# Clustered attention and two MLPs on one core: which engine copies which transposes, and when ScalarE converts weights

## The chip, the core and the metric

The kernel runs on one core of one Trainium2 chip. A core has TensorE (PE in the profile, its weight loads PEld), VectorE (DVE), ScalarE (ACT), GpSimd (POOL) and SyncE (SP), each with a queue of its own that runs in order, and 16 DMA engines. The metric is the device time of one execution in microseconds.

## The reference, cut to what matters

```
q, k, v: (2, 8, 768, 64);  centroids: (8, 16, 64)
q_assign, k_assign = argmax of normalized q, k times normalized centroids
scores = q k^T / 8, and -1e9 where the two assignments differ
attn   = softmax(scores);  x = attn v, reshaped to (1536, 512)
h = x @ w_in (512 x 2048);   x = (h * sigmoid(h)) @ w_out
gate = sigmoid(x @ w_gate (512 x 1536));  val = x @ w_val
out = (gate * val) @ w_out2 (1536 x 512)
```

The weights come as 64-bit floats and are turned into 32-bit floats on the chip. All results are fp32.

## The kernel before

**Attention.** The 16 heads are handled in eight pairs p of two heads j, and the 768 queries of a head in six tiles i of 128; one pair is thus twelve tiles, called 0 to 11 below. `one_tile` runs two tiles ahead with `scores`: four matmuls into one of two PSUM buffers `s`, VectorE's maximum over the row (L462), and ScalarE's exponential into `e` (L467), which also sums. `transposes` (L481 and L492) then turns the 128 x 768 block of `e` by six TensorE transposes: two go into a tile `u` that two query tiles share, four into a tile `t`. Both kinds of tile come from one PSUM pool of three buffers. A copy moves them to the SBUF tile `ph`; it is written in the helper `cast`, so its line is L64 on ScalarE and L67 on VectorE. VectorE copies each shared `u`. After every third tile `values` (L500) multiplies by v for the three tiles before; ScalarE copies one half of the result (`other`, L509) and VectorE adds the other (L512). `finish_last` scales the last pair's result into `acc`.

**Weights.** A job makes the operands of one weight block. `converted` loads 64-bit words (L687), and turns them into floats by ScalarE (L692), GpSimd (L693) and three steps of bits on VectorE (L698, L700, L702). `two` splits a float into a high part, cast by ScalarE (again L64), and the rest, subtracted by GpSimd (L710). `seven` makes the seven operands of a Strassen scheme: GpSimd forms the sums `si` and `two` splits them, for the first block into `wi0a`, `wi0b`, `wi0s`, `wi0t`. `plain` makes a block of the output weights (`wo`). The jobs stand in one list: first hidden block, its two output blocks, second hidden block, and so on. `weights(key)` traces a job and the two behind it.

**MLPs.** `hidden` runs a hidden block of the first MLP by Strassen's scheme in steps x, w, X, y, z, v, W; the first block runs it for one half of the tokens and `hidden_directly` for the other. `mixed` multiplies by the output weights; in its first pass ScalarE copies the product to `acc` (L901), and in later ones VectorE adds (L903). The second MLP follows in the same manner.

**What sets the order.** In the long loops TensorE's instructions keep the order of the code (`manual_schedule`). For the other engines a planner decides from simulated times and the order of the code which ready instruction comes next, and so it does for the PSUM buffer that a tile gets; the chip then runs each queue in that order. `tc.issue_after(ins)` keeps the instructions of a block behind `ins`, if they are on the engine of `ins`. `begin` holds the exponential of the last pair's first tile; `ends` the last value copy L509 (and a matmul). `behind` does this for VectorE's bit steps of the first four conversions.

The code that the diff touches:

Of the kernel before, what the change touches and what calls it, by code (L numbers as in the profile page):

```python
# [14 lines left out]
AF = mybir.ActivationFunctionType  # L15
# [16 lines left out]
def clustered_attention_then_two_mlps(ctx, tc, qT, kT, v, cen, cenT, w1i, w1o, w2g, w2v, w2o, out):  # L32
    nc = tc.nc
    B, HP, _, S = qT.shape
# [10 lines left out]
    NPAIR = B * HP  # L45
# [3 lines left out]
    GT = G // P  # L49
# [6 lines left out]
    ends = []  # L56
    begin = []
    maxima = []
    copied = []
    home = {0: xp}  # L60

    def cast(eng, o, i):
        if eng is nc.scalar:
            return nc.scalar.activation(o, i, AF.Copy)  # L64
        if eng is nc.gpsimd:
            return nc.gpsimd.tensor_scalar(o, i, 1.0, 1.0, op0=ALU.mult, op1=ALU.mult)
        return nc.vector.tensor_copy(o, i)  # L67
# [41 lines left out]
    with ExitStack() as att:  # L109
# [339 lines left out]
        def scores(p, j, i):  # L449
            qa, qm, ka, km, _ = heads[p]  # L450
            s = ps_s.tile([P, 2, 512], F32, tag="s", name=f"s{p}_{j}_{i}")
            for n, (a, c) in enumerate(((qa, ka), (qm, km))):
                for g in range(2):
                    nc.tensor.matmul(  # L454
                        s[:, g, 0:HS],
                        lhsT=a[:, j, i * P : (i + 1) * P],
                        rhs=c[:, j, g * HS : (g + 1) * HS],
                        start=n == 0,
                        stop=n == 1,
                    )  # L460
            nm = sm.tile([P, 1], F32, tag="nm", name=f"nm{p}_{j}_{i}")
            maxima.append(nc.vector.tensor_reduce(nm, s[:, :, 0:HS], axis=AX.XY, op=ALU.max, negate=True))  # L462
            e = wk.tile([P, 2, HS], F32, tag="e", name=f"e{p}_{j}_{i}", bufs=4)
            if p not in tots:
                tots[p] = fin.tile([P, 2 * NT], F32, tag="tot", name=f"tot{p}")
            n = j * NT + i
            x = nc.scalar.activation(e, s[:, :, 0:HS], AF.Exp, bias=nm, scale=1.0, accum_out=tots[p][:, n : n + 1])  # L467
            if (p, j, i) == (NPAIR - 1, 0, 0):
                begin.append(x)
            prob[p, j, i] = e  # L470

        ring = wk.tile([P, NT, S], F32, tag="ph", name="ph", bufs=1)
# [2 lines left out]
        def transposes(p, j, i):  # L475
            e = prob.pop((p, j, i)).rearrange("p a b -> p (a b)")
            if i % 2 == 0:
                shared[0] = ps_t.tile([P, 2, 2, P], F32, tag="t", name=f"u{p}_{j}_{i}")
            both = shared[0]
            for kt in (4, 5):  # L480
                nc.tensor.transpose(both[:, kt - 4, i % 2, :], e[:, kt * P : (kt + 1) * P], ident)  # L481
            if i % 2:
                copied[:] = [
                    cast(
                        nc.vector,
                        ring[:, 4:6, (i - 1) * P : (i + 1) * P],
                        both.rearrange("p k i q -> p k (i q)"),
                    )
                ]
            t = ps_t.tile([P, 4, P], F32, tag="t", name=f"t{p}_{j}_{i}")  # L490
            for kt in range(4):
                nc.tensor.transpose(t[:, kt, :], e[:, kt * P : (kt + 1) * P], ident)  # L492
            eng = nc.vector if i % GT == 1 and p < NPAIR - 1 else nc.scalar
            cast(eng, ring[:, 0:4, i * P : (i + 1) * P], t)

        def values(p, j, g):
# [102 lines left out]
        for t in tiles[:2]:  # L599
            scores(*t)  # L600
# [57 lines left out]
        for i in (NT - 2, NT - 1):  # L658
            transposes(p, 1, i)
# [23 lines left out]
    def converted(src, name):  # L683

        r = rp.tile([P, KD * P], mybir.dt.int64, tag="r", name=f"r{name}")
        with tc.issue_after(loaded[0].ins):
            nc.sync.dma_start(r, src)  # L687
        words = r.bitcast(I32).rearrange("p (n w) -> p n w", w=2)
        low, up_ = words[:, :, 0], words[:, :, 1]
        t = wp.tile([P, KD * P], F32, tag="c", name=f"c{name}")  # L690
        ti = t.bitcast(I32)
        nc.scalar.activation(t, up_.bitcast(F32), AF.Copy, scale=2.0**-112)  # L692
        nc.gpsimd.tensor_scalar(t, t, LARGEST, -LARGEST, op0=ALU.min, op1=ALU.max)  # L693
        def one():
            return tc.issue_after(behind.pop(0).ins) if behind else nullcontext()

        with one():
            nc.vector.tensor_scalar(ti, ti, 3, None, op0=ALU.logical_shift_left)  # L698
        with one():
            nc.vector.scalar_tensor_tensor(ti, low, 29, ti, op0=ALU.logical_shift_right, op1=ALU.bitwise_or)  # L700
        with one():
            nc.vector.scalar_tensor_tensor(ti, up_, SIGN, ti, op0=ALU.bitwise_and, op1=ALU.bitwise_or)  # L702
        return t

    def two(src, name, pool=None):

        w = (pool or sp[next(taken) % NSP]).tile([P, 2, src.shape[1]], R32, tag="w", name=f"w{name}")
        hi, lo = w[:, 0], w[:, 1]
        cast(nc.scalar, hi, src)
        nc.gpsimd.tensor_tensor(lo, src, hi, op=ALU.subtract)  # L710
        return hi, lo

    def plain(src, name):
        return two(converted(src, name), name)

    def four(srcs, name):

# [9 lines left out]
    def part(pair, n):  # L727
        return [h[:, n * Q : (n + 1) * Q].rearrange("p (k c) -> p k c", k=KQ) for h in pair]

    def seven(srcs, name, all_four=False):  # L730

        a, b = (converted(src, f"{name}_{n}") for n, src in enumerate(srcs))
        a11, a12, a21, a22 = a[:, 0:Q], a[:, Q:], b[:, 0:Q], b[:, Q:]
        first = two(a, f"{name}a")
        t = wp.tile([P, 4, Q], F32, tag="s", name=f"s{name}", bufs=1)
        sub = nc.gpsimd.tensor_tensor
        sub(t[:, 0], a21, a22, op=ALU.add)
        sub(t[:, 1], t[:, 0], a11, op=ALU.subtract)
        sub(t[:, 2], a11, a21, op=ALU.subtract)
        sub(t[:, 3], a12, t[:, 1], op=ALU.subtract)  # L740
        s12 = two(t[:, 0:2].rearrange("p a b -> p (a b)"), f"{name}s")
        s34 = two(t[:, 2:4].rearrange("p a b -> p (a b)"), f"{name}t")
        last = two(b, f"{name}b") if all_four else two(a22, f"{name}d", dp)
        made = dict(
            a11=part(first, 0),
            a12=part(first, 1),
            s1=part(s12, 0),
            s2=part(s12, 1),
            s3=part(s34, 0),
            s4=part(s34, 1),  # L750
            a22=part(last, 1 if all_four else 0),
        )
        if all_four:
            made["a21"] = part(last, 0)
        return made

    jobs, place = [], {}

    def job(key, make, *args):
        place[key] = len(jobs)  # L760
        jobs.append(partial(make, *args))

    def flat(w):
        return w.rearrange("p k c -> p (k c)")

    for i in range(N1):
        job(("1i", i), seven, [flat(w1i[2 * i + n]) for n in range(2)], f"i{i}", i == 0)
        for e in range(2):
            job(("1o", i, e), plain, w1o[i, e], f"o{i}_{e}")
    for i in range(N2):  # L770
        job(("2g", i), seven if i else four, [flat(w2g[2 * i + n]) for n in range(2)], f"g{i}")
        job(("2v", i), seven if i else four, [flat(w2v[2 * i + n]) for n in range(2)], f"v{i}")
# [1 line left out]
            job(("2o", i, k), plain, flat(w2o[2 * i + k]), f"u{i}_{k}")  # L774

    AHEAD = 2
    made = {}

    def weights(*key):

        n = place[key]
        for c in range(n, min(n + AHEAD + 1, len(jobs))):
            if c not in made:
                with tc.issue_after((ends if c > AHEAD else begin)[0].ins):
                    made[c] = jobs[c]()
        return made[n]

# [95 lines left out]
    def hidden(i, bs, order="xyzwXvW"):  # L883
        def take(c, m, h, bs, inside):
            g = c if inside else temporary(f"g{i}_{m}{h}{bs.start}")[:, bs]
            nc.scalar.activation(g, c, AF.Silu)
            split(g, m, (h, bs), f"a{i}", nc.gpsimd if m and h else nc.vector)

        yield from strassen(weights("1i", i), f"h{i}", take, bs, order)
# [8 lines left out]

    def accumulate(z, o, first):
        if first:  # L900
            nc.scalar.activation(z, o, AF.Copy)  # L901
        else:
            nc.vector.tensor_tensor(z, o, z, op=ALU.add)  # L903

# [125 lines left out]
    def steps(main, beside=iter(()), n=None):  # L1030

        for _ in main:
            next(beside, None)
            if n is not None:
                n -= 1
                if n == 0:
                    return
# [26 lines left out]
    for q in ("21", "22"):  # L1064
        right_quarter("x", 1, q, ACT, DVE)
    front = hidden(0, ONE[0], "xwXyzvW")
    steps(front, n=6)
    following = hidden_directly(0, 1)
    next(following)
    run(front)  # L1070
# [90 lines left out]
```

## Time and profile before

| | |
|---|---|
| median of three runs | 783.1 us (782.8 to 783.15) |
| profiled execution | 783.0 us, span 781.1 us |
| TensorE busy | 765.1 us, 98% (weight loads 83%) |
| VectorE, ScalarE, GpSimd busy | 80%, 52%, 51% |
| TensorE's clock granted | full, in all 40 slices |
| TensorE's longest waits in total | 4.2 us for the exponential (18 times), 1.4 for ScalarE's copies to acc |

A row of the timeline has the start from the beginning of the span, the length, the engine, the line, the operation with output and inputs, the shape and how many were merged. In brackets stand the idle time of the engine ahead of it and what ended it. Buffer numbers are left out of names: `s`, `t`, `u`, `v` are PSUM tiles of attention, `e` the exponentials, `ph` the transposed ones, `ci` and `co` the floats of hidden and output weights, `ri` and `ro` their loaded words. A row of the busy table has a stretch, its length, and the busy time and number of instructions of each engine.

### The profile page before, as it was taken

The page shows a single profiled execution, that of the slowest core. Times are in us where ns is not written, and L with a number is a line of the kernel's source. Part 1 is how long each engine was busy: PE and PEld are TensorE (multiplying, and loading weights), DVE is VectorE, ACT ScalarE, POOL GpSimd, SP SyncE. Part 2 cuts the span into 40 slices and gives each one's busy share as a digit, 9 for nine tenths or more (in the row PEclk, how much of TensorE's full clock was granted, in tenths as well). Part 3 has the DMA queues.
Part 4 walks back from the last instruction along what each step waited for, and adds up shares of the span by engine and source line. Part 5 has one row for each costly group of instructions (what it writes and reads, how often), then busy time and mean ns, then how long its engine had stood idle before and what let it go on. Part 6 is the DMA issues. An engine that isn't in the chain of part 4 may idle for free.

```text
span 781.1 us, 11455 instructions
## 1 busy us (share of the span) xinstructions
PE 765.1 (98%) x4314; PEld 651.9 (83%) x4314; DVE 626.9 (80%) x787; ACT 403.1 (52%) x690; POOL 396.2 (51%) x345
## 2 busy tenths in 40 slices
PE   8999999999998999999999999999999999999998
PEld 4666776666766988989989989998998989899896
DVE  6887887787777989979678678998497896979746
ACT  6767777777785754615525326546532425333120
POOL 5234223556654776646546326445663847748220
PEclk9999999999999999999999999999999999999999
DMA  7675466367221132222121211221021221112004
GB/s 215 154 184 146 120 164 167 111 150 196 81 75 55 54 134 83 81 81 81 55 81 55 81 55 55 81 76 58 31 81 55 81 82 54 55 68 68 1 0 162
DMA packets 25487, 71.60 MB, mean 92 GB/s; under 512 B 4484, under 2 KB 4952, under 8 KB 25432
## 3 DMA queue, kind: packets, MB, share of 16 engines
q1 hardware_dynamic: 24888, 70.84, 30.7%
q8 instruction: 34, 0.56, 0.3%
q14 instruction: 21, 0.17, 0.1%
q10 hardware_dynamic: 544, 0.03, 0.0%
HBM read 48.01 MB, written 3.19 MB: 66 GB/s over the span
## 4 chain that ended last, share of the span: by engine, by line
PE 79%; DVE 9%; ACT 6%; issue 2%; DMA 2%; POOL 1%; SPq 0%; ACTq 0%; POOLq 0%; DVEq 0%
PE z L982 12%; PE v L500 7%; PE s L454 7%; PE t L492 4%; PE h_0w L807 3%; PE h_0x L807 3%; ACT e L467 3%; PE g_0w L807 2%; PE g_0x L807 2%; PE u L481 2%; PE y_00None L923 2%; PE v_0w L807 2%; PE v_0x L807 2%; PE r L873 2%; PE q L873 2%
## 5 line engine op out<-in xcount | busy, mean ns | idle before, releaser
L462 DVE TENSOR_REDUCE nm<-s 128x1 f32<-128x768 f32 x96 | 91.5, 954 | 18.6 <-PE s L454 18.0
L467 ACT ACTIVATE e<-s,nm 128x768 f32<-128x768 f32 x96 | 86.5, 901 | 28.2 <-DVE nm L462 27.4
L982 PE MATMUL z<-wu,ghb 128*128 128x512 f32 (+1 forms) x292 | 89.7, 389 | 0.5 <-DVE acc L903 0.5
L500 PE MATMUL v<-ph,vv 128*64 128x384 f32 x384 | 69.2, 494 | 0.3 <-DVE ph L67 0.3
L982 PEld LDWEIGHTS z<-wu,ghb 128*128 128x128 f32 x292 | 54.0, 188 | 12.5 <-issue 1.3
L454 PE MATMUL s<-ka,qa 128*128 128x384 f32 x192 | 57.6, 380 | 4.3 <-ACT e L467 4.2
L492 PE MATMUL t<-ident,e 128*128 128x128 f32 x384 | 58.1, 274 | 0.3
L982 PE MATMUL z<-wu,glb 128*128 128x512 f32 (+1 forms) x146 | 57.0, 391 | 0.0
L531 POOL TENSOR_TENSOR acc<-xf,rb 128x768 f32<-128x768 f32 x7 | 12.8, 1835 | 82.6 <-DMA rb<-d_rb 82.6
L64 ACT ACTIVATE ph<-t 128x512 f32<-128x512 f32 x68 | 40.6, 599 | 21.7 <-PE t L492 20.9
L500 PEld LDWEIGHTS v<-ph,vv 128*64 128x64 f32 x384 | 25.2, 136 | 30.6 <-issue 22.9
L454 PE MATMUL s<-k,q 128*128 128x384 f32 x192 | 49.8, 339 | 0.1
L903 DVE TENSOR_TENSOR acc<-z,acc 128x1024 f32<-128x1024 f32 (+2 forms) x32 | 36.6, 1154 | 13.6 <-PE z L982 12.9
L492 PEld LDWEIGHTS t<-ident,e 128*128 128x128 f32 x384 | 43.9, 140 | 2.4 <-ACT ph L64 2.2
L481 PEld LDWEIGHTS u<-ident,e 128*128 128x128 f32 x192 | 22.8, 140 | 26.2 <-issue 19.2
L67 DVE COPY ph<-u 128x512 f32<-128x512 f32 x48 | 32.8, 684 | 12.7 <-PE u L481 12.7
L481 PE MATMUL u<-ident,e 128*128 128x128 f32 x192 | 38.8, 283 | 1.1 <-ACT ph L64 1.1
L454 PEld LDWEIGHTS s<-ka,qa 128*128 128x128 f32 x192 | 28.9, 190 | 9.8 <-ACT e L467 9.0
L710 POOL TENSOR_TENSOR wo<-co,wo 128x512 fp32r<-128x512 f32 x16 | 23.2, 1452 | 23.8 <-ACT wo L64 23.7
L454 PEld LDWEIGHTS s<-k,q 128*128 128x128 f32 x192 | 34.5, 188 | 0.8 <-ACT k L333 0.3
L982 PEld LDWEIGHTS z<-wu,glb 128*128 128x128 f32 x146 | 27.4, 188 | 7.3 <-DVE glb L863 1.8
L923 PE MATMUL y<-gha,wo 128*128 128x384 f32 x128 | 32.8, 334 | 0.0
(626 smaller groups left out, 2133.0 us busy)
## 6 DMA issues: line engine op xcount, KB each, us to landing
ri<-in_w1i SPq DMA_DIRECT2D x16, 512.0 KB, 3.2
ro<-in_w1o SPq DMA_DIRECT2D x16, 512.0 KB, 3.3
ka<-kh SPq DMA_DIRECT2D x32, 192.0 KB, 3.9
rg<-in_w2g SPq DMA_DIRECT2D x12, 512.0 KB, 3.2
rv<-in_w2v SPq DMA_DIRECT2D x12, 512.0 KB, 3.1
ru<-in_w2o SPq DMA_DIRECT2D x12, 512.0 KB, 3.3
qq<-in_qT SPq DMA_DIRECT2D x8, 384.0 KB, 3.3
kk<-in_kT SPq DMA_DIRECT2D x8, 384.0 KB, 4.8
```

What stands on the lines that cost most here:

```text
L64: return nc.scalar.activation(o, i, AF.Copy)
L67: return nc.vector.tensor_copy(o, i)
L454: nc.tensor.matmul(s[:, g, 0:HS], lhsT=a[:, j, i * P : (i + 1) * P], rhs=c[:, j, g * HS : (g + 1) * HS], start=n == 0, stop=n == 1,)
L462: maxima.append(nc.vector.tensor_reduce(nm, s[:, :, 0:HS], axis=AX.XY, op=ALU.max, negate=True))
L467: x = nc.scalar.activation(e, s[:, :, 0:HS], AF.Exp, bias=nm, scale=1.0, accum_out=tots[p][:, n : n + 1])
L481: nc.tensor.transpose(both[:, kt - 4, i % 2, :], e[:, kt * P : (kt + 1) * P], ident)
L492: nc.tensor.transpose(t[:, kt, :], e[:, kt * P : (kt + 1) * P], ident)
L500: m = nc.tensor.matmul(o[(L, U)[kt % 2]], lhsT=vv[:, j, kt, :], rhs=ring[:, kt, g * G : (g + 1) * G], start=n < 2, stop=n >= NT - 2,)
L807: nc.tensor.matmul(o[:, b, 0:HS], lhsT=w[a][s][:, k, :], rhs=right[b, q][t][:, k, :], start=start and k == 0 and n == 0, stop=k == KQ - 1 ...
L903: nc.vector.tensor_tensor(z, o, z, op=ALU.add)
L923: nc.tensor.matmul(o[:, d, 0:width], lhsT=s[:, d, k, :], rhs=t[:, c], start=k == 0 and m == 0, stop=k == 1 and m == 2,)
L982: nc.tensor.matmul(o[:, a, c], lhsT=s[:, q * P : (q + 1) * P], rhs=r[:, c], start=k == 0 and m == 0, stop=k == 1 and m == 2, skip_group_ch ...
```

## The change

VectorE copies the `t` tile of query tiles 1 and 3 of each half pair instead of 1 and 4; the others stay with ScalarE, and in the last pair all do. For the first hidden block the casts of the two operands of sums are put behind the latest exponential, which is the last one when they are traced. For the first block's output weights the high casts are put behind the last value copy, and their two jobs are traced after the first step of the first hidden block instead of ahead of all of them. All ScalarE instructions of the third hidden block's job are put behind the latest copy L901 traced by then, the last of the first output pass; before, they stood behind the value copy.

```diff
-    copied = []
+    copied, latest, firsts = [], [], []
...
             x = nc.scalar.activation(e, s[:, :, 0:HS], AF.Exp, bias=nm, scale=1.0, accum_out=tots[p][:, n : n + 1])
...
+            latest[:] = [x]
...
-            eng = nc.vector if i % GT == 1 and p < NPAIR - 1 else nc.scalar
+            eng = nc.vector if i in (1, GT) and p < NPAIR - 1 else nc.scalar
             cast(eng, ring[:, 0:4, i * P : (i + 1) * P], t)
...
-    def two(src, name, pool=None):
+    def two(src, name, pool=None, after=()):
...
-        cast(nc.scalar, hi, src)
+        with tc.issue_after(after[0].ins) if after else nullcontext():
+            cast(nc.scalar, hi, src)
         nc.gpsimd.tensor_tensor(lo, src, hi, op=ALU.subtract)
...
-    def plain(src, name):
-        return two(converted(src, name), name)
+    def plain(src, name, after=()):
+        return two(converted(src, name), name, after=after)
...
-        s12 = two(t[:, 0:2].rearrange("p a b -> p (a b)"), f"{name}s")
-        s34 = two(t[:, 2:4].rearrange("p a b -> p (a b)"), f"{name}t")
+        after = latest if all_four else ()
+        s12 = two(t[:, 0:2].rearrange("p a b -> p (a b)"), f"{name}s", after=after)
+        s34 = two(t[:, 2:4].rearrange("p a b -> p (a b)"), f"{name}t", after=after)
...
-            job(("1o", i, e), plain, w1o[i, e], f"o{i}_{e}")
+            job(("1o", i, e), plain, w1o[i, e], f"o{i}_{e}", () if i else ends)
...
     AHEAD = 2
+    look = [0]
...
-        for c in range(n, min(n + AHEAD + 1, len(jobs))):
+        for c in range(n, min(n + look[0] + 1, len(jobs))):
             if c not in made:
-                with tc.issue_after((ends if c > AHEAD else begin)[0].ins):
+                behind_it = firsts if c == place["1i", 2] else ends if c > AHEAD else begin
+                with tc.issue_after(behind_it[0].ins):
                     made[c] = jobs[c]()
...
         if first:
-            nc.scalar.activation(z, o, AF.Copy)
+            firsts[:] = [nc.scalar.activation(z, o, AF.Copy)]
...
-    steps(front, n=6)
+    steps(front, n=1)
+    look[0] = AHEAD
+    weights("1i", 0)
+    steps(front, n=5)
```

## Rows read from the trace of the kernel before

**Rows 1.** Timeline, 79.4 to 82.2 us, a first half pair.
```profile
79.52 0.96 DVE L462 TENSOR_REDUCE nm<-s 128x1 f32<-128x768 f32 x1 [0.15 <-PE s L454]
...
80.28 0.60 ACT L64 ACTIVATE ph<-t 128x512 f32<-128x512 f32 x1 [0.39 <-PE t L492]
80.39 0.68 DVE L67 COPY ph<-u 128x512 f32<-128x512 f32 x1
...
80.78 0.90 ACT L467 ACTIVATE e<-s,nm 128x768 f32<-128x768 f32 x1
...
80.94 0.43 PEld L492 LDWEIGHTS t<-ident,e 128*128 128x128 f32 x4
80.99 0.96 DVE L462 TENSOR_REDUCE nm<-s 128x1 f32<-128x768 f32 x1
...
81.82 0.30 PEld L454 LDWEIGHTS s<-ka,qa 128*128 128x128 f32 x2 [0.45 <-ACT e L467]
...
82.05 0.90 ACT L467 ACTIVATE e<-s,nm 128x768 f32<-128x768 f32 x1 [0.28 <-DVE nm L462]
```

**Rows 2.** Timeline, 92 to 96 us, a second half pair.
```profile
93.20 0.96 DVE L462 TENSOR_REDUCE nm<-s 128x1 f32<-128x768 f32 x1 [0.23 <-PE s L454]
...
94.08 0.68 DVE L67 COPY ph<-u 128x512 f32<-128x512 f32 x1
...
94.35 0.90 ACT L467 ACTIVATE e<-s,nm 128x768 f32<-128x768 f32 x1
...
95.39 0.30 PEld L454 LDWEIGHTS s<-ka,qa 128*128 128x128 f32 x2 [0.45 <-ACT e L467]
```

**Rows 3.** Timeline, 231 to 237 us, the end of attention.
```profile
231.46 0.68 ACT L692 ACTIVATE co<-ro 128x512 f32<-128x512 f32 x1 [1.06 <-POOL wi0b L710]
...
232.15 0.63 ACT L64 ACTIVATE wi0s<-si 128x512 fp32r<-128x512 f32 x1
...
232.69 0.89 ACT L467 ACTIVATE e<-s,nm 128x768 f32<-128x768 f32 x1
...
233.57 0.62 ACT L64 ACTIVATE wi0t<-si 128x512 fp32r<-128x512 f32 x1
...
234.21 0.49 ACT L509 ACTIVATE other<-v 64x384 f32<-64x384 f32 x1
...
236.80 2.16 PE L500 MATMUL v<-ph,vv 128*64 128x384 f32 x12 [0.28 <-DVE ph L67]
```

**Rows 4.** Timeline, 243 to 251 us, the first hidden block.
```profile
243.88 1.25 ACT L64 ACTIVATE wo<-co 128x512 fp32r<-128x512 f32 x2 [3.44 <-DVE co L702]
243.92 0.94 SPq L687 DMA_DIRECT2D ri<-in_w1i  x2
...
246.21 1.00 PEld L807 LDWEIGHTS h_0x<-x,wi0a 128*128 128x128 f32 x6 [0.80 <-ACT h_0u L828]
...
247.19 0.66 ACT L692 ACTIVATE ci<-ri 128x512 f32<-128x512 f32 x1 [1.04 <-DMA ri<-in_w1i]
...
250.10 1.01 PEld L807 LDWEIGHTS h_0v<-xt,wi0b 128*128 128x128 f32 x6 [0.82 <-DVE h_0u L830]
```

**Rows 5.** Busy time by stretches, the one from 246 to 299 us.
```profile
246.00:299.00 53.00, 50.24 (x283) 48.92 (x284) 48.49 (x53) 36.26 (x57) 36.48 (x31) 1.00 0.26 92
```

**Rows 6.** Timeline, 277 to 299 us, the second hidden block.
```profile
277.41 0.67 ACT L692 ACTIVATE ci<-ri 128x512 f32<-128x512 f32 x1 [1.94 <-DMA ri<-in_w1i]
...
278.82 0.43 DVE L698 TENSOR_SCALAR ci<-ci 128x512 int32<-128x512 int32 x1 [0.67 <-POOL ci L693]
...
282.73 1.28 POOL L710 TENSOR_TENSOR wi2a<-ci,wi2a 128x512 fp32r<-128x512 f32 x1
282.80 1.50 DVE L698 TENSOR_SCALAR ci<-ci 128x512 int32<-128x512 int32 x1 [1.14 <-POOL ci L693]
283.34 2.04 PEld L807 LDWEIGHTS h_0z<-xt,wi1t 128*128 128x128 f32 x12 [1.74 <-ACT acc L901]
...
298.82 0.47 PE L923 MATMUL y_00None<-gha,wo 128*128 128x512 f32 x1 [0.64 <-DVE h_0u L846]
```

## The prediction

> **What bounds the kernel now.** The page's first part comes first: TensorE is busy for nearly the whole span, VectorE for four fifths, ScalarE for half. So little can be won, and only in the idle time of TensorE. The second part shows it at full clock in every slice, so the clock is no term here. The view of waits for TensorE is second: its idle time is one wait repeated in the attention stage, the score matmuls waiting for an exponential, and single waits around the first hidden block. The timeline of all engines at these places is third, and the busy table by stretches last.
>
> The repeated wait has a chain that can be read off one place. Scores go into two PSUM buffers, so the scores of tile 7 of a pair of heads (twelve tiles, 0 to 11) need the exponential of tile 5. The maximum of tile 5 runs on VectorE from 79.52 to 80.48, ScalarE copies the fourth tile's transposes from 80.28 to 80.88, the exponential starts only at 80.78 and runs 0.90, and the weight load of the scores follows at 81.82 after 0.45 of idling [rows 1]. An exponential whose ScalarE is free starts 0.10 behind its maximum (81.95 to 82.05); this one starts 0.30 behind it [rows 1]. The second half of each pair repeats it for tile 11: maximum done at 94.16, exponential at 94.35, so 0.19 behind [rows 2]. These two places come back at the same offsets in every pair from the second to the seventh; in the first pair only the second place waits, and in the eighth all these copies stay on ScalarE.
>
> At the end of attention the exponential of tile 10 of the last pair starts at 232.69, behind two weight conversions on ScalarE (231.46, 0.68 and 232.15, 0.63); a third (233.57, 0.62) stands between it and the value copy at 234.21, and the value product that waits on this chain starts at 236.80 [rows 3]. Next ScalarE holds two output-weight casts that wait 3.44 for VectorE, from 243.88 to 245.13; the value copy and the first hidden block's copy queue behind them, and TensorE idles 0.80 at 246.21. Then ScalarE waits 1.04 for a weight load that was issued at 243.92, and VectorE's sum comes late: 0.82 at 250.10 [rows 4]. (These are the weight-load rows; the matmul rows give somewhat less, since their ends are modelled.)
>
> From 246 to 299 VectorE is busy 48.49 of 53.00 us [rows 5]. TensorE's waits there are mostly VectorE's backlog seen from the other side. The largest, 1.74 at 283.34, is a PSUM bank that ScalarE releases late, since its queue stood 1.94 at a weight conversion waiting for its load (277.41). The next, 0.64 at 298.82, is VectorE's queue itself [rows 6].
>
> **The change, part by part.** The sum is made against the profiled execution, 783.0 us (span 781.1 and 1.9 around it); the median of the runs is 783.1.
>
> *The transposes' copies.* In each half pair VectorE copied tiles 1 and 4 of six; now it copies 1 and 3, and ScalarE takes 4. The counts stay, so no engine gets more work; what moves is place. ScalarE is free when tile 5's maximum ends, and the exponential starts 0.10 behind it: 0.30 - 0.10 = 0.20 in six pairs, and 0.19 - 0.10 = 0.09 in seven second halves. 6 x 0.20 + 7 x 0.09 = 1.8 us, on the path, since the scores follow that exponential 0.14 later both times [rows 1, 2]. The cover has to be checked on VectorE: after the maximum it copies the pair of shared transposes (80.39 to 81.07) and now tile 3's behind it, to 81.75 with the same 0.68. That pushes the next maximum (80.99) by 0.7 at most; its exponential is needed only behind the value product that comes next. But the transposes of the next tile need one of three PSUM buffers. Now they start at 80.94, 0.06 behind ScalarE's copy. With that copy gone the first buffer free is the shared one, 81.07 + 0.06 = 81.13, and with 0.43 for the four loads the scores could start at 81.56, where the new exponential allows 81.62. In the second half it is 94.76 + 0.06 + 0.43 = 95.25 against 95.30. So the saving just fits. The best case is no more: maximum and exponential in sequence set it. The other end is a rival.
>
> *Two casts behind the last exponential.* Without the cast at 232.15 the exponential starts 0.64 earlier (0.09 before the end of the conversion ahead of it, as it does now), and without the one at 233.57 the value copy gains another 0.64. Sum 1.28. The value product at 236.80 hangs on this chain through VectorE's queue [rows 3]. The casts go behind tile 11's exponential, where ScalarE and GpSimd have gaps; their first user is the block ahead of 246.21, over five us later. Taken: 1.3. If the conversion at 231.46 also leaves (its job is now traced later), another 0.7 goes; if the planner puts other conversions in the gap, 0.
>
> *Output-weight casts behind the last value copy.* This frees the copy of the first hidden block, so the 0.80 at 246.21 can go, and the 0.82 at 250.10 with it if the split of the attention result starts earlier. I price this at nothing beyond the shift of 1.3, because that split (ScalarE, behind 247.19) waits for a load issued when VectorE finishes the output weights' bit operations [rows 4], and these are shifted by 1.3, not removed. Upper end 0.80 + 0.82 = 1.6; below nothing by the collision weighed next.
>
> A gap that the casts leave may be filled by their GpSimd halves. The same VectorE shift of 128x512 words took 0.43 at 278.82 and 1.50 at 282.80, where it began 0.07 behind a GpSimd subtraction of 1.28 and ended 0.3 behind it [rows 6]. So one GpSimd subtraction can cost VectorE 1.07, and the two that move may land on the bit operations ahead of 243.92: up to 2.1. The Trainium skill (SBUF — State Buffer, Who interferes with whom) says that the port pair the two share is locked for a whole instruction by whichever starts first; this row agrees, and by that rule the edit puts work on VectorE's own path. The front's lower end is 1.3 - 2.1 = -0.8.
>
> *Third job's conversions behind the second layer's copies.* ScalarE then releases the bank as soon as its product is done, and the 1.74 at 283.34 goes. But the next stop is the wait at 298.82, which VectorE sets [rows 6]. VectorE's own idle time between is 0.67 and 1.14, both ahead of conversion steps that need loads; the conversion at 277.41 itself moves back about 0.9. One sum (about 0.9) can now slip into the 1.14, less about 0.5 for the later conversion: 0.4 taken. Ends: 1.74 + 0.64 = 2.4 if VectorE's backlog dissolves, 0 if nothing slips in. So the 1.74 mostly turns into a longer wait at 298.82.
>
> Sum: 1.8 + 1.3 + 0.4 = 3.5; 783.0 - 3.5 = 779.5. Nothing behind 299 has a reason to change: there the same jobs run in the same order, and what is gained is carried along.
>
> **The rivals.**
> *Everything pays.* VectorE's backlog between 246 and 299 shrinks with the earlier start: 1.8 + 1.3 + 1.6 + 2.4 = 7.1, so 775.9. For it: 4.5 us of idle VectorE in that stretch [rows 5]. Against: its idle is ahead of loads, not of TensorE.
> *The front is swallowed.* The collision above, or conversions planned into the gap, take the 1.3: 783.0 - 1.8 - 0.4 = 780.8, and 781.6 with the whole 2.1.
> *The edit does not reach the exponential.* The planner may set another ScalarE instruction in the freed slot, or VectorE's maximum may come later: the 1.8 stays away, and with the front swallowed too only 0.4 is left, 782.6. Against: the slot holds nothing else now.
> *Slower: the transposes wait for VectorE's second copy.* If the fifth tile's transposes get the buffer of the fourth tile, they wait for 81.75 + 0.06, scores at 82.24 instead of 81.82, +0.42; in the second half 94.76 + 0.68 + 0.06 + 0.43 = 95.93 instead of 95.39, +0.54. 6 x 0.42 + 7 x 0.54 = 6.3 lost in place of 1.8 won: 783.0 + 6.3 - 1.7 = 787.6. It decides from a copy that ends later than about 81.33. For it: the saving has only some 0.05 us of room. Against: buffers are now taken in the order in which they come free, not in fixed rotation (at 80.94 one freed at 80.88, with the shared one still in use until 81.07) [rows 1].
>
> **How the numbers follow.** Forecast 779.5: 0.50, own range 778.3 to 780.6. Everything pays: 0.13. Front swallowed: 0.18. No reach: 0.11. Slower: 0.08. A measurement of this kernel tells about 0.2% from no change, 1.6 us, so faster means under 781.4 or so: 0.50 + 0.13 + 0.13 of the swallowed case = 0.76. Within: the rest of that case and most of no reach, 0.15. Slower 0.09. The range 776.2 to 782.8 leaves out the slower rival and the far half of the best one.
>
> **What would show it.** Right: the score waits of six first halves shrink from 0.45 to about 0.25 and a pair takes 0.3 less; the value product stands 1.3 earlier against the scores of tile 11; the wait at the bank of 283.34 is gone and the one before the second layer's second pass has grown. Wrong: transposes of the fifth tile start over 0.4 behind the shared copy; a VectorE row of the output weights' bit operations over 1.4 long; the time from the last exponential to the second layer's second pass as long as now, or over 4 us shorter.

## The result, and the profile after

The changed kernel is slower: median 788.17 us (786.99 to 788.51, four runs) against 783.12 (782.8 to 783.16) before, ratio 1.0063 [1.0045, 1.008]. The profiled execution took 788.4, span 786.6. The forecast was 779.5. The first 295 us went better than forecast; then one stop of TensorE and what followed it gave back twice what had been won. In the names below `p` is the product of the half of the tokens that the first block multiplies directly, `gha` and `gla` are the high and the low part of a Silu's result, and `y_00` is the first product of the second layer's second pass. A negative shift is earlier.

```
start of the same work on TensorE   before   after    shift
transposes, end of attention        235.37   231.38   -3.99
first hidden block, h_0v            250.10   244.81   -5.29
direct products p                   251.28   247.39   -3.89
second hidden block, h_0z           283.34   278.45   -4.89
third hidden block, h_0x            293.86   288.85   -5.01
third hidden block, h_0y            295.94   295.90   -0.04
second layer, y_00                  298.82   300.86   +2.04
y_00, seven products on             300.62   303.69   +3.07
third hidden block, h_0z            315.36   319.93   +4.57
```

The first edit did what it should. The timeline of the changed kernel at the place of [rows 1], and two rows at that of [rows 2]:

```profile
78.53 0.96 DVE L462 TENSOR_REDUCE nm<-s 128x1 f32<-128x768 f32 x1 [0.16 <-PE s L454]
...
79.41 0.68 DVE L67 COPY ph<-u 128x512 f32<-128x512 f32 x1
...
79.52 0.90 ACT L467 ACTIVATE e<-s,nm 128x768 f32<-128x768 f32 x1 [0.62 <-DVE nm L462]
...
80.14 0.42 PEld L493 LDWEIGHTS t<-ident,e 128*128 128x128 f32 x4 [0.19 <-DVE ph L67]
...
80.57 0.30 PEld L454 LDWEIGHTS s<-ka,qa 128*128 128x128 f32 x2
...
93.55 0.42 PEld L493 LDWEIGHTS t<-ident,e 128*128 128x128 f32 x4 [0.31 <-DVE ph L67]
...
93.98 0.30 PEld L454 LDWEIGHTS s<-ka,qa 128*128 128x128 f32 x2
```

The exponential starts 0.03 behind its maximum (79.49 to 79.52). The scores at 80.57 wait for nothing now; the transposes ahead of them wait for the shared copy, 0.05 behind its end (80.09), as reckoned. From one tile's scores to the next it was 1.81 and is 1.56 in first halves and 1.66 in second halves, so a pair takes 0.4 less. Behind the last of these places, at 209 us, the scores stand 2.85 earlier (208.51 before, 205.66 now). Of that 0.25 was there at the scores of 14.96 us already (14.71 now), ahead of the first copy that moved, so the edit gave 2.6.

The front, at the place of [rows 3, 4]:

```profile
230.22 0.49 ACT L510 ACTIVATE other<-v 64x384 f32<-64x384 f32 x1
...
232.80 0.20 PEld L501 LDWEIGHTS v<-ph,vv 128*64 128x64 f32 x4 [0.27 <-DVE ph L67]
...
241.58 0.99 PEld L812 LDWEIGHTS h_0x<-x,wi0a 128*128 128x128 f32 x6
...
243.40 0.66 ACT L693 ACTIVATE ci<-ri 128x512 f32<-128x512 f32 x1 [0.83 <-DMA ri<-in_w1i]
...
245.56 1.28 ACT L891 ACT_TABLE_LOAD   x1
...
246.85 0.49 ACT L891 ACTIVATE g<-h_0x 128x384 f32<-128x384 f32 x1
...
247.39 4.44 PE L878 MATMUL p<-x,wi0a 128*128 128x384 f32 x24 [1.38 <-ACT g L891]
```

Value copy and value product stand 3.99 and 4.00 earlier. The last scores of attention stood 2.88 earlier (232.70 before, 229.82 now), so the front brought 1.1 up to there, a little less than the 1.28 of the forecast. The stalls of 0.80 and 0.82 went as well, and at h_0v the front has 2.4. But p now waits 1.38 for the first Silu, and 1.0 is left. That Silu stands on ScalarE behind the conversion that waits for its load; directly ahead of it stands a table load of ScalarE of 1.28, which the kernel before has at the same place and which no run here moved.

The place that decides, ScalarE, VectorE, GpSimd and TensorE around [rows 6]:

```profile
274.88 0.63 ACT L64 ACTIVATE wo<-co 128x512 fp32r<-128x512 f32 x1 [2.84 <-DVE co L703]
275.41 2.20 ACT L906 ACTIVATE acc<-y 128x768 f32<-128x768 f32 x3
277.49 1.41 ACT L693 ACTIVATE ci<-ri 128x512 f32<-128x512 f32 x2
...
278.45 2.24 PE L812 MATMUL h_0z<-xt,wi1t 128*128 128x384 f32 x12
...
278.90 0.43 DVE L699 TENSOR_SCALAR ci<-ci 128x512 int32<-128x512 int32 x1 [4.05 <-POOL ci L694]
...
288.99 2.31 POOL L868 TENSOR_TENSOR gla<-h_0d,gha 128x768 fp32r<-128x768 f32 x1
...
291.25 1.44 POOL L740 TENSOR_TENSOR si<-si,ci 128x256 f32<-128x256 f32 x1
...
293.27 0.63 ACT L64 ACTIVATE wo<-co 128x512 fp32r<-128x512 f32 x1 [2.01 <-DVE co L703]
...
295.23 0.62 ACT L64 ACTIVATE wi2s<-si 128x512 fp32r<-128x512 f32 x1
...
295.90 1.65 PE L812 MATMUL h_0y<-xt,wi2s 128*128 128x384 f32 x4 [4.81 <-ACT wi2s L64]
...
296.61 1.46 POOL L712 TENSOR_TENSOR wi2s<-si,wi2s 128x512 fp32r<-128x512 f32 x1
...
298.13 2.93 PE L812 MATMUL h_0y<-xt,wi2s 128*128 128x384 f32 x8 [0.58 <-POOL wi2s L712]
...
300.86 0.63 PE L928 MATMUL y_00None<-gha,wo 128*128 128x512 f32 x1
```

The bank wait of 1.74 at h_0z is gone, as meant. Both conversions now stand behind the eighth copy; VectorE, whose bit steps follow them, idles 4.05. What stands last in this chain is the operand wi2s: GpSimd forms its sum (L740) behind the 2.31 of another block's subtraction. The sum is done at 292.69, but the cast comes only at 295.23, since ScalarE stands 2.01 at a cast wo that waits for VectorE, and then runs two more instructions first. The low part ends at 298.07, and TensorE waits 4.81 and 0.58. The busy table of the changed kernel (stretch, length, busy time and instructions of PE, PEld, DVE, ACT, POOL; then the granted clock, DMA share, GB/s):

```profile
246.00:299.00 53.00, 45.73 (x254) 44.57 (x254) 46.67 (x50) 34.52 (x54) 33.08 (x28) 0.95 0.21 70
...
273.00:286.00 13.00, 12.50 (x72) 12.18 (x72) 8.74 (x12) 5.95 (x10) 4.00 (x4) 1.00 0.28 92
286.00:299.00 13.00, 7.61 (x37) 6.79 (x36) 12.20 (x10) 9.78 (x16) 12.61 (x11) 0.78 0.24 82
...
296.00:303.00 7.00, 6.42 (x18) 5.43 (x19) 6.93 (x8) 2.42 (x4) 5.71 (x5) 0.50 0.08 14
```

Against [rows 5] TensorE and GpSimd did less in the 53 us. GpSimd's share is the telling one: 4.00 of 13 us to 286, then 12.61 of 13. And the clock, full throughout before, is at 0.50 from 296 to 303, so at 1.2 in place of 2.4 GHz, right behind TensorE's long idle stretch. From h_0x to h_0z TensorE loses 9.6 us against the kernel before: 4.97 at the wait for the cast, 2.08 to the start of y_00 (0.58 of waiting and slow products, less the 0.64 that was waited there before), 1.03 in y_00, 1.50 at h_0z, which now waits 1.34 for VectorE's sum. Over the whole span the loss is 5.5 (781.1 to 786.6).

### The profile page after: what moved, and what is told of

It is laid out like the page before. It is cut to its first block, busy times and chain, and to the rows that moved or that the text cites. A ratio compares the mean times of both kernels' runs of the same rounds, so it can differ in the third digit from the quotient of the medians.

```text
span 786.6 us, 11463 instructions
## 1 busy us (share of the span) xinstructions
PE 767.1 (98%) x4313; PEld 654.4 (83%) x4314; DVE 627.9 (80%) x787; ACT 404.4 (51%) x690; POOL 394.7 (50%) x345
## 4 chain that ended last, share of the span: by engine, by line
PE 76%; DVE 12%; ACT 4%; issue 3%; DMA 2%; POOL 1%; ACTq 0%; SPq 0%; POOLq 0%; DVEq 0%
PE z L987 12%; PE v L501 7%; PE s L454 7%; PE t L493 4%; PE h_0w L812 3%; PE h_0x L812 3%; PE g_0w L812 2%; PE g_0x L812 2%; PE u L482 2%; PE v_0w L812 2%; PE v_0x L812 2%; PE r L878 2%; PE q L878 2%; PE y L928 2%; PE y_00None L928 2%
## 5 line engine op out<-in xcount | busy, mean ns | idle before, releaser
L712 POOL TENSOR_TENSOR wo<-co,wo 128x512 fp32r<-128x512 f32 x16 | 20.7, 1299 | 27.8 <-ACT wo L64 27.8
```

## Experiments

Theory A: the third edit takes a conversion from a place where it hid, and all that hangs on it (VectorE's bits, GpSimd's sums) comes too late. Theory B: TensorE simply comes earlier and would have waited for these weights anyway. Theory C: a part of the loss is TensorE's clock. Theory D: VectorE's amount of work sets the pace from 246 to 299. Effects in us are ratios times 783.

**Without the third edit.**

```
-                behind_it = firsts if c == place["1i", 2] else ends if c > AHEAD else begin
+                behind_it = ends if c > AHEAD else begin
```

> The changed kernel without its third edit: the third hidden block's conversions stand behind the value copy again, all else stays. Theory A (the moved job): holding these conversions behind the last copy to acc lets VectorE idle 4.05 us and makes the operand wi2s late; without the edit the wait of TensorE at h_0y for wi2s falls from 4.81 to under 1.5 us, TensorE's clock stays full, and the time is 778 to 780.5. Theory B (TensorE came too early): the conversions cannot be ready sooner whatever stands ahead of them, so the 5 us saved ahead of this place are waited for there; the wait stays at 4 to 5 us with the half clock behind it, 785 to 788.

Measured: 780.03 (779.41 to 780.5), ratio 0.9965 [0.9953, 0.9978], the clock full. So the third edit costs 0.0098, 7.7 us, on top of the other two. The same place in its timeline:

```profile
273.62 0.68 ACT L693 ACTIVATE ci<-ri 128x512 f32<-128x512 f32 x1 [1.94 <-DMA ri<-in_w1i]
...
274.53 0.64 ACT L64 ACTIVATE wo<-co 128x512 fp32r<-128x512 f32 x1 [0.23 <-DVE co L703]
...
275.07 1.50 ACT L906 ACTIVATE acc<-y 128x768 f32<-128x768 f32 x2
...
287.30 0.62 ACT L64 ACTIVATE wi2s<-si 128x512 fp32r<-128x512 f32 x1
...
289.25 1.74 POOL L712 TENSOR_TENSOR wi2s<-si,wi2s 128x512 fp32r<-128x512 f32 x1
290.95 2.29 POOL L868 TENSOR_TENSOR gla<-h_0d,gha 128x768 fp32r<-128x768 f32 x1
...
295.07 0.47 PE L928 MATMUL y_00None<-gha,wo 128*128 128x512 f32 x1 [0.94 <-DVE h_0u L851]
```

The conversion stands at 273.62, inside a stretch in which ScalarE has to wait for VectorE's co anyway. Held back, it leaves one wait of 2.84 ahead of the cast wo where there are 1.94 and 0.23 here, and the sixth and seventh copies to acc start no earlier for it (275.41 held, 275.07 here). Only the eighth does, ahead of which the second conversion no longer stands: h_0z waits 0.99 for it here and not at all there. The price grows from queue to queue. Against this kernel, which is 0.3 ahead at the second block's h_0x (273.17 against 273.51), the changed one has VectorE's last bit step 3.8 later (done 285.86 against 282.09), the sum L740 6.6 later (292.69 against 286.12) and the cast of wi2s 7.9 later. GpSimd's two stretches here, the same as above:

```profile
273.00:286.00 13.00, 11.50 (x65) 10.87 (x65) 10.88 (x14) 6.94 (x11) 8.24 (x9) 1.00 0.35 122
286.00:299.00 13.00, 12.06 (x64) 10.89 (x64) 11.90 (x11) 10.19 (x16) 12.24 (x10) 1.00 0.25 83
```

So the hold pushed 4.2 us of GpSimd's work (8.24 less 4.00) and 2.1 of VectorE's over 286, into a stretch in which GpSimd is full.

**The first edit alone, the second alone, the third alone.** (Each is the kernel before with one of the edits from the diff above.)

> The kernel before with the first edit alone (VectorE copies tiles 1 and 3). Both theories: the exponentials of tiles 5 and 11 start 0.2 to 0.3 and 0.1 to 0.15 earlier, the attention stage is 2.4 us shorter, and since the weight conversions of the last pair hang on the same exponentials, everything behind moves with it: 780.4 to 781.0. If theory B held for this edit too (conversions bound by loads that do not move), up to 1.3 us of it would show as a wait at wi2s: 781.7 or more.

> The kernel before with the second edit alone (two casts behind the last exponential, output-weight casts behind the last value copy, their jobs traced later). Theory A: the front of the first hidden block is 1.3 to 2.6 us shorter and keeps it, 780.3 to 781.8. Theory B: the gain is waited for at wi2s, 782.5 to 783.5.

> The kernel before with the third edit alone (the third hidden block's conversions behind the last copy to acc). Theory A: the bank wait of 1.74 us at h_0z goes, but wi2s comes 3 to 4 us later than before, so TensorE waits for it 2 to 5 us, and if its clock falls again the time is 784 to 788. Theory B: without the earlier arrival there is no such wait, 782 to 783.5.

Measured: first 780.46 (779.94 to 782.24), 0.9975 [0.9966, 0.9984]; second 782.78 (782.11 to 783.08), 0.9998 [0.9989, 1.0007]; third 789.46 (788.62 to 790.78), 1.0087 [1.0073, 1.0101]. The first came as expected. The second lies 1.0 above A's range and in B's, but TensorE does not wait for wi2s there, as B would have it. The third lies 1.5 above A's range. The three effects, -2.0, -0.2 and +6.8, add up to 4.6; all together measured 4.9. The third alone shows the same stop although TensorE is not early (its timeline):

```profile
282.21 0.43 DVE L698 TENSOR_SCALAR ci<-ci 128x512 int32<-128x512 int32 x1 [4.05 <-POOL ci L693]
...
299.00 1.65 PE L808 MATMUL h_0y<-xt,wi2s 128*128 128x384 f32 x4 [4.59 <-ACT wi2s L64]
```

That refutes B: the weights are late, TensorE isn't early. In the kernel with the second edit alone, the gain of the front is 2.3 at h_0v, 0.7 at p and 0.1 at y_00 (without the 0.21 by which this execution is early from attention on). Most of it ends at p:

```profile
250.39 4.46 PE L878 MATMUL p<-x,wi0a 128*128 128x384 f32 x24 [1.64 <-ACT g L891]
...
298.50 0.47 PE L928 MATMUL y_00None<-gha,wo 128*128 128x512 f32 x1 [0.98 <-DVE h_0u L851]
```

**The clock's part.** Between h_0x and h_0y of the third block TensorE multiplies what nobody reads, 26 times, in the time in which it would wait:

```
-                add(c["u2"], run(bank(f"{name}y"), "s2", "t2"), c["u2"])
+                oy = bank(f"{name}y")
+                if name == "h2_0":
+                    for n_ in range(26):
+                        nc.tensor.matmul(
+                            oy[:, 0, 0:HS], lhsT=w["a11"][0][:, 0, :], rhs=right[0, "11"][0][:, 0, :], start=True, stop=True
+                        )
+                add(c["u2"], run(oy, "s2", "t2"), c["u2"])
```

> The changed kernel with 26 extra matmuls of 128x384 into the bank of the product that waits for wi2s, ahead of its first real matmul; they are overwritten. Theory C (part of the loss is TensorE's clock): the extra matmuls fill the 4.81 us wait, the granted clock stays at its full level between 290 and 304, and the eleven or so matmuls that took twice as long behind the wait are fast: 1.5 to 3 us less than the changed kernel, 785 to 786.7. If the clock had no price, the time stays at 787.5 to 788.5.

Measured: 784.91 (783.4 to 785.98), 1.003 [1.0019, 1.0042]: 0.0033 less than with all three edits, 2.6 us, within the 1.5 to 3 that C expected. The operand wi2s comes as late (cast at 294.70, low part to 297.57), but its timeline and busy table show full speed behind it:

```profile
297.63 1.66 PE L812 MATMUL h_0y<-xt,wi2s 128*128 128x384 f32 x8 [1.29 <-POOL wi2s L712]
```
```profile
296.00:303.00 7.00, 5.71 (x27) 4.71 (x27) 6.96 (x6) 1.88 (x4) 5.71 (x5) 1.00 0.12 46
```

The eight products take 1.66 instead of 2.93. So of the 7.7 us the clock is about a third, and it is lost only because TensorE stops.

**A looser hold.** The third block's job behind the sixth copy instead of the eighth; and, in another kernel, without the third edit, only its second conversion behind the last copy:

```
-                behind_it = firsts if c == place["1i", 2] else ends if c > AHEAD else begin
+                behind_it = firsts[5:] if c == place["1i", 2] else ends if c > AHEAD else begin
...
-            firsts[:] = [nc.scalar.activation(z, o, AF.Copy)]
+            firsts.append(nc.scalar.activation(z, o, AF.Copy))
```
```
-        nc.scalar.activation(t, up_.bitcast(F32), AF.Copy, scale=2.0**-112)
+        with tc.issue_after(firsts[0].ins) if name == "i2_1" else nullcontext():
+            nc.scalar.activation(t, up_.bitcast(F32), AF.Copy, scale=2.0**-112)
```

> The changed kernel with the third hidden block's conversions behind the sixth of the eight copies to acc in place of the eighth. Theory A in its dose: the first conversion starts about 2 us later than without a hold and 2 us earlier than with the full one; VectorE's idle time ahead of it is 2 to 3 us in place of 4.05, wi2s is ready before TensorE asks for it or up to 2 us late, 779.5 to 783. If the order in the queues behind it, not the late start, makes wi2s late, the wait stays above 4 us and the time above 786.

> The changed kernel without its third edit, and only the second of the third hidden block's two conversions on ScalarE stands behind the last copy to acc. That conversion waits for its load anyway (1.28 us), so the copy can go ahead of it. Theory A: the bank wait at h_0z (1.0 us) goes, wi2s is not late, and since VectorE's queue sets the next stop, 0 to 0.8 us of it is kept: 779.2 to 780.2. If any hold behind the last copy is what costs: 783 or more.

Measured: sixth copy 783.77 (782.12 to 785.71), 1.0026 [1.0015, 1.0037]; second conversion 783.04 (781.49 to 783.98), 1.0009 [1.0, 1.0018]. Theory A expected both faster. The sixth copy lies above its 779.5 to 783 and below the 786 of the other case; the second conversion came out as the other case said, 783 or more. In both wi2s is in time (low part done by 288.8 and 289.5, used after 291), yet y_00 waits, for VectorE in the end. After the sixth copy, and after the second conversion:

```profile
291.41 1.66 DVE L701 SCALAR_TENSOR_TENSOR co<-ro,co 128x512 int32<-128x512 int32 x1
292.99 0.94 DVE L845 TENSOR_TENSOR h_0u<-h_0u,h_0v 128x768 f32<-128x768 f32 x1
...
296.65 0.47 PE L928 MATMUL y_00None<-gha,wo 128*128 128x512 f32 x1 [2.73 <-ACT gha L64]
```
```profile
293.42 2.32 DVE L704 SCALAR_TENSOR_TENSOR co<-ro,co 128x512 int32<-128x512 int32 x1
...
297.08 0.80 PE L929 MATMUL y_00None<-gla,wo 128*128 128x512 f32 x1 [2.52 <-DVE gla L869]
```

Each time VectorE's queue holds bit steps of output weights ahead of the sum or subtraction that y_00 needs. With the second conversion held, h_0z starts 1.3 us earlier (277.99 against 279.26), and y_00 loses more than that.

**Less work on VectorE.** Without the third edit, and without the last two bit steps for the second block's output weights (these lack low bits and sign):

```
+        if name not in ("o1_0", "o1_1"):
+            with one():
+                nc.vector.scalar_tensor_tensor(ti, low, 29, ti, op0=ALU.logical_shift_right, op1=ALU.bitwise_or)
+            with one():
+                nc.vector.scalar_tensor_tensor(ti, up_, SIGN, ti, op0=ALU.bitwise_and, op1=ALU.bitwise_or)
```

> The changed kernel without its third edit, and with four of VectorE's steps left out (the last two bit steps of the second hidden block's two output-weight conversions, about 3.7 us on VectorE between 265 and 275), so these weights lack their low bits and sign. It asks why the second edit gains nothing. Theory D (VectorE's queue sets the pace from 246 to 299): TensorE's waits at p, y, z and y_00 (3.8 us together) shrink by 1.5 to 3 us, 777 to 778.5. If TensorE or the loads set it: 779.5 to 780.3, unchanged.

Measured: 779.16 (778.88 to 781.71), 0.9966 [0.9954, 0.9979], by the ratio the same as with them (0.9965). VectorE idles instead, behind ScalarE, which itself stands behind casts that wait for VectorE:

```profile
280.59 0.96 DVE L836 TENSOR_TENSOR h_0u<-h_0y,h_0u 128x768 f32<-128x768 f32 x1 [2.44 <-ACT h_0u L834]
```

So D's gain did not come. The run is a weak test of it, though. VectorE's busy time from 246 to 299 fell by 1.2 us and not by 3.7 (48.47 with the steps, 47.23 without), since other steps took longer (two at L76 4.02 at 265.59, 1.81 with the steps) and later work moved up. The planner changed the order too: the third block's first conversion starts at 266.97 in place of 273.62. That the order in the queues sets the pace there fits the row above, but no run shows it.

**The order behind the hold.** All three edits with their hold; the third block's job is traced ahead of the second block, and GpSimd's subtraction gla of h_0d is put behind the third block's sums (first kernel; summed holds L742), or behind the low part of wi2s as well (second kernel; summed holds that subtraction):

```
-        parted[:] = [subber.tensor_tensor(lo, src, hi, op=ALU.subtract)]
+        with tc.issue_after(summed[0].ins) if summed and subber is nc.gpsimd and i == "a1" else nullcontext():
+            parted[:] = [subber.tensor_tensor(lo, src, hi, op=ALU.subtract)]
...
+    weights("1o", 1, 0)
     run(hidden(1, ALL))
```

> The changed kernel, all three edits, with the third block's weight sums (L740, L742 on GpSimd) put ahead of the second block's subtraction gla of h_0d, which stood 2.31 us ahead of L740 there; the hold behind the eighth copy stays. If the queue order behind the late start carries most of the loss, the cast of wi2s comes near 291.5 instead of 295.23 and its low part near 294 instead of 298.07, TensorE's wait of 4.81 shrinks to about 1 to 2.5, the clock stays full or falls for less long, and the time is 781.5 to 785. If the late start alone carries it (VectorE's 4.05 us of idling, not made up whatever the order behind it), VectorE's queue sets the pace, the wait only moves to y_00, and the time stays at 786.5 to 788.5.

> As the kernel with the sums first (785.96), and GpSimd's subtraction gla of h_0d stands behind the low part of wi2s too. There GpSimd was busy without a gap from 286.05 to 299, with wi2s at 294.99, and TensorE waited 3.57 us for it. If the order of GpSimd's queue is the whole loss, wi2s is done near 292.7, TensorE waits about 1 us and the time is 780 to 782.5. If GpSimd's work that the hold put off (busy 3.76 us of the 13 from 273 to 286, 8.24 without the third edit) has to be done then in any order, gla of h_0d comes 2 to 3 us later instead, the wait moves to the second layer's product behind it, and the time stays at 784 to 786.5.

Measured: sums first 785.96 (785.0 to 786.47), 1.0045 [1.0033, 1.0058], between the two ranges (781.5 to 785 if order is most of the loss, 786.5 to 788.5 if the late start is); low part first 781.94 (781.13 to 783.99), 0.9998 [0.9989, 1.0007], in the range of order. The second one:

```profile
291.09 0.63 ACT L64 ACTIVATE wi2s<-si 128x512 fp32r<-128x512 f32 x1
...
292.48 1.27 POOL L712 TENSOR_TENSOR wi2s<-si,wi2s 128x512 fp32r<-128x512 f32 x1
293.71 2.54 POOL L871 TENSOR_TENSOR gla<-h_0d,gha 128x768 fp32r<-128x768 f32 x1
...
293.80 2.34 PE L814 MATMUL h_0y<-xt,wi2s 128*128 128x384 f32 x8 [1.07 <-POOL wi2s L712]
```

The conversion starts as late as in the changed kernel and VectorE idles the same 4.06. What differs is the order behind it: on GpSimd by the edit, and on ScalarE too, where the planner now has the cast of wi2s (291.09) ahead of the cast wo that waits for VectorE, and not behind it (295.23). With that 0.0065 of the 0.0098 is back: 5.1 of 7.7 us, a share of the clock's loss among them. With the sums alone ahead ScalarE has the same order in this stage (cast at 291.10), yet TensorE still waited 3.57 for the low part, behind gla and a conversion step; so 0.0047, 3.7 us, hang on the place of the low part in GpSimd's queue. The other 1.4 us, of the sums and ScalarE's cast, are within the intervals of the two runs. What is left, 0.0033 or 2.6 us, is the late start itself or another order that was not tried; the two runs don't tell these apart.

**Two attempts to do better**, both on the kernel without the third edit: its third job traced earlier (the line weights("1o", 1, 0) from above alone), and the second block's job on ScalarE behind the first Silu, to free p:

```
-                behind_it = ends if c > AHEAD else begin
+                behind_it = silus if c == place["1i", 1] else ends if c > AHEAD else begin
...
-            nc.scalar.activation(g, c, AF.Silu)
+            silus.append(nc.scalar.activation(g, c, AF.Silu))
```

> The kernel without the third edit (780.0), with the third hidden block's job traced ahead of the second hidden block instead of behind it, so that the planner prefers its instructions. If queue order is what sets the pace between 277 and 300, this moves the time by up to 2 us either way: 778 to 782. If the amount of work on VectorE sets it, it stays at 780.0 within 0.5.

> The kernel without the third edit (780.0), with the second hidden block's weight conversions on ScalarE held behind the first Silu, so that the copy's successor g does not wait for a load. If ScalarE's order ahead of Silu g is what gives back the second edit's gain, the direct products p start 0.5 to 1.5 us earlier and the time falls to 778.5 to 779.7. If VectorE and the later waits (0.5 at h_0y, 1.0 at h_0z) swallow it, the time is 779.8 to 780.5; if the later start of VectorE's bit steps makes the second block's weights late, as the third edit did to the third's, it is over 782.

Measured: traced earlier 779.34 (779.16 to 781.1), 0.997 [0.9959, 0.9981], no different. Its trace has the instructions of ScalarE, VectorE and GpSimd in the same order in this stage as without the line, so the attempt moved nothing and tells nothing about order. (It does show that this line, which the two kernels above have too, reorders nothing by itself without the hold.) Behind the Silu 783.9 (781.29 to 785.56), 1.0021 [1.0012, 1.0031], slower by 0.0056. There p starts 1.50 earlier, as hoped, so it did wait for that Silu; a wait of 1.87 in the first output pass takes it back, and the second hidden block starts 1.04 later than without the edit (274.21 against 273.17):

```profile
265.95 0.45 PE L928 MATMUL y<-gla,wo 128*128 128x384 f32 x1 [1.87 <-DVE gla L868]
```

The second block's weights are not late (cast of wi1s at 258.72, 261.87 without the edit), so the third case has the time right but not the path. Its profiled execution, 781.3, is the fastest of its twelve and the only one whose mean granted clock is 1.0; in the others it is 0.995 to 0.998, so the clock fell somewhere in them, which is not in that trace. The version to keep is the one without the third edit: 0.35% under the kernel before, 1.0% under the changed one. The runs do not tell it from the first edit alone (0.9965 [0.9953, 0.9978] and 0.9975 [0.9966, 0.9984]).

## Why the prediction was wrong

*What bounds it.* Right for the score waits. "The clock is no term here" held for the kernel before, but not behind the stop that the edit made; the clock cost about 2.6 us. "Nothing behind 299 has a reason to change" did not hold either: the loss at y_00 of 2.04 was 4.57 by h_0z.

*The transposes' copies, 1.8.* Right in mechanism and order of waits, and somewhat low: 2.6 in the trace, because the exponential starts 0.03 to 0.04 behind the maximum where 0.10 was taken from an exponential with a free ScalarE. Alone the edit is worth 2.0 us. The slower rival (transposes that wait for the second copy, decided at 81.33) did not come: they waited for the shared copy, and the buffer came free at the moment that was worked out.

*Two casts behind the last exponential, 1.3.* Of the 1.28, 1.1 was there at the value product, and the stalls of 0.80 and 0.82, priced at nothing, went too. Yet alone the edit is worth 0.2 us, not distinguishable from nothing. The step that failed is that the gain is carried along: p had stood close behind the first Silu before, and that Silu hangs on a load and on ScalarE's queue. The prediction asked what is late next only up to h_0v. The swallowed case came true, by this wait and a longer one at y_00 and not by the collision on GpSimd.

*Third job behind the second layer's copies, 0.4, ends 2.4 to 0.* This is the step that decided. Its working was that ScalarE's 1.94 at the conversion would go, that the conversion "moves back about 0.9", and that the worst case is nothing gained. First, the 1.94 was not ScalarE's to win: the cast wo behind it waits for VectorE until the same moment. In the kernel before the sixth and seventh copies start at 278.72, in the changed one at 275.41. That is 3.31 earlier, less than the 3.81 by which TensorE is early at h_0x (277.32 and 273.51), so h_0y now waits 0.50 for a copy. Second, so the conversion moved back from 274.10 (277.41 less the 3.31) to 277.49, by 3.4 and not 0.9. Third, a conversion has a chain behind it, which for wi2s passes five times from engine to engine, and the sum priced only its first step. VectorE's 4.05 of idling could not be made up, because GpSimd has no room behind 286, and in-order queues put another 2.31 ahead of the sum on GpSimd and a cast that waits for VectorE ahead of the cast on ScalarE. Measured: +7.7 on top of the other two edits, +6.8 alone. The forecast should have held a loss: the slack of that chain could have been read from the trace before (low part of wi2s done at 294.73, h_0y begun at 295.94, so 1.2, and a little more since the first four products of h_0y wait for the cast alone), and 3.4 is more than that.

The Trainium skill (PSUM — Partial Sum Buffer, Engine vs sequencer instructions) calls the queues of ScalarE, VectorE and GpSimd strict FIFO. The traces agree: L740 starts when the 2.31 of gla end (291.25), though its inputs were there from 287.4 on, when GpSimd's first sum (L739) ended.

## What to carry to other kernels

Before an instruction is held back, read what its engine would do in the time that comes free: if it would wait there for something else, the hold gains nothing there and delays everything behind the instruction. Follow the held instruction to the last consumer of its chain on every in-order queue, and compare the delay with the slack of that consumer; an engine that is full afterwards cannot make up what it idles now. A stall that goes is worth something only if the next wait on the path is not set by a load or a queue that has not moved.

## What the runs showed of the hardware that was not expected

The clock's fall does not follow from the length of one wait as the profile lists it. Behind waits of 4.81 and 0.58 the granted clock was 0.50 over 296 to 303. In the profiled execution of the kernel held to the sixth copy, behind a wait of 2.73 at y_00, it stayed full; in that of the one with the second conversion held, behind 2.52 after four short products, it was lower (the busy tables of these two, in this order):

```profile
296.00:303.00 7.00, 5.94 (x25) 4.65 (x26) 6.85 (x9) 3.46 (x5) 1.97 (x3) 1.00 0.19 71
```
```profile
296.00:303.00 7.00, 5.92 (x20) 4.79 (x21) 6.17 (x8) 1.10 (x2) 2.65 (x3) 0.76 0.20 75
```

With the low part first, two waits of about 1 us (0.78 and 1.07) were followed by 0.86 over the same stretch. The same kernel can go either way: held to the sixth copy, the mean granted clock was 1.0 in the profiled execution and 0.996 to 0.998 in the six others; with the low part first it was 0.997 in the profiled one and 0.999 or 1.0 in the eleven others. So one trace does not tell whether a kernel with such stops keeps its clock. Why, no run here shows. A second point: in the profiled execution, products that nobody reads, 26 of them in 4.67 us, kept the clock full over 296 to 303, and the cast of wi2s and the first real product behind it came no later for them.
